# Another way of turning a 128-row tile upside down, and a later place for the transform that reads it

## The chip, the cores and the metric

The kernel runs on one core of one Trainium2 chip. The metric is device time in microseconds (us) of one launch, from the first to the last instruction of the program and a little around it. The engines are PE (matrix multiplications, with PEld for its weight loads), DVE, ACT and POOL (elementwise work) and SP, which here only issues DMA transfers. Each engine works through its own list of instructions in order; semaphores make it wait for others.

## The reference, cut to what matters

Three stages follow each other on a batch of 2 sequences of 768 tokens with 512 features. The first is a linear attention with decay (blocks of 64 tokens). The second is this, and the change lies in it:

```
X = np.fft.fft(x, axis=1)            # over the 768 tokens
X = np.fft.fft(X, axis=2)            # over the 512 features
mixed = np.real(X)
u = x + mixed
un = (u - mean(u)) / sqrt(var(u) + 1e-06)
x = u + np.maximum(un @ w_ch1, 0.0) @ w_ch2      # 512 -> 2048 -> 512
```

The third is a second MLP of the same size with its own normalisation. All inputs and outputs are float32; the kernel carries most products as pairs of float16 (a high part and the rest).

## The kernel before, in words

The tokens of a sequence are cut into six tiles of 128. `U[b][j]`, j from 0 to 5, holds the attention's output of sequence b; tiles 3 to 5 hold the mirrored half of the tokens. The real part of a two-dimensional Fourier transform is symmetric, so the kernel adds and subtracts mirrored tokens and mirrored features first ("fold") and multiplies by smaller cosine and sine tables. For sequence 1 it folds once more over the tokens: tile 0 of the folded rows is added to and subtracted from tile 2 with its rows in reverse order. This reversed copy is the tile `turned` (z in the code): row 0 of z is zero, and row p is row 128 - p of the folded tile 2. [...] `fold_mid` (L585) folds tile 1, `fold_both` (L588 to L595) folds tile 0, copies half a row into it (L590), and makes `radd` and `rsub` (L593); each is split into a float16 pair `fadd`, `fsub` by ACT (L563) and POOL (L564).

`dft1_two` (L609 to L636) multiplies these pairs by the token tables, in five groups g of output columns (L622, L627, L630), and ACT and DVE copy the sums out as `cst` (L635, L636). `dft2_q` (L672) and `dft2_x` (L656, L658) transform over the features into `ps_pq`, three tiles j, and `add_cos` (L691) adds the result to U. Then come the statistics (L777 to L796), the normalised rows `un` and their pair `uns` (L797 to L806), and a DMA transpose into `unT` (L808), from which the MLP's first product of block 2 reads.

This work runs beside the MLP of the blocks that are ready. The MLP is cut into units n of one block and one sixteenth of the 2048 features: `mlp_up` (L843) makes `ps_h`, ACT and DVE turn it into the pair h (L857, L858), and `mlp_down`, three units later, multiplies h by the second weights into `ps_y` (L1003). A table `bg` says which background task is emitted in which unit: `put(n, task)` rounds n down. A task emitted there is a piece of program; a scheduler then sets the order on PE, DVE, ACT and POOL by its own estimate of times, and instructions may end up somewhat before or after their unit. DMA issues that wait for nothing on an engine can stand much earlier. SP issues all transfers of this part in one list, and waits in it for the data of each.

The lines that set the places are these (L1455 to L1464):

```
n = t + DC + DFO                 # 22
put(n - 2, fold_turn)
put(n, fold_mid)
put(n, fold_both)
n += DD                          # 22.5
for i, g in enumerate((2, 3, 4, 0, 1)):
    put(n + i * D1S, lambda g=g: dft1_two(g, bk1))     # D1S = 0.5
n += 4 * D1S + 1
```

`w1_sums` (L876 to L888) prepares sums of the first weights on DVE, ACT and POOL and has no part in the transform; its instructions `wr`, `ws` and `sw` stand between the others.

Of the kernel before, what the change touches and what calls it, by code (L numbers as in the profile page):

```python
# [11 lines left out]
F32 = mybir.dt.float32  # L12
# [7 lines left out]
P = 128  # L20
B, H, S, D = 2, 8, 768, 64
DM, DF = 512, 2048
# [29 lines left out]
EARLY0, GATEN, B1, SPC, DS, DC, DFO, DD, D1S, D2S, AO, YA, NR, NE, LN1, L1, L2, F01, F02, TL, R1, R2, SE, PR1, LAG, UB, FB, NW, MQ, SPL = 11, 8, 6, 2.0, 2.0, 5, 1.0, 0.5, 0.5, 1.0, "aba", "aa", 2, 0, 3, 2.5, 2.5, 16, 4, 3, 1.5, 2, "dddd_dppp", 0, 3, 3, 13, 11, 1, 3  # L52
# [22 lines left out]
def split16(a):  # L75
    hi = a.astype(np.float16)
    lo = (a - hi.astype(np.float64)).astype(np.float16)
    return hi, lo


def shape_tables():
    t = np.arange(TB)
    s = np.arange(NS)
    ang = 2.0 * np.pi * ((t[:, None] * s[None, :]) % S) / S
    cs = np.cos(ang) * TS
    sn = np.sin(ang) * TS
    d = np.arange(P)
    dd = np.arange(ND)
    cd = np.cos(2.0 * np.pi * ((d[:, None] * dd[None, :]) % DM) / DM) * TS
    dse, dso = d[:, None] * dd[None, 2:-1:2], (d[:, None] + 1) * dd[None, 1::2]  # L90
    sd = np.sin(2.0 * np.pi * (np.concatenate([dso, dse], 1) % DM) / DM) * TS
    sd[P - 1, :P] *= 0.5

    def lay(a, n):
        parts = [x.reshape(n, P, -1).transpose(1, 0, 2) for x in split16(a)]
        return np.ascontiguousarray(np.stack(parts, 1))

    def full(a, n):
        return np.ascontiguousarray(a.astype(np.float32).reshape(n, P, -1).transpose(1, 0, 2))

    even, odd = np.arange(0, DM, 2), np.arange(1, DM, 2)
    wide = np.stack([np.cos(2.0 * np.pi * (d[:, None] * even % DM) / DM), np.cos(2.0 * np.pi * (d[:, None] * odd % DM) / DM),
                     -np.sin(2.0 * np.pi * (d[:, None] * even % DM) / DM), -np.sin(2.0 * np.pi * ((d[:, None] + 1) * odd % DM) / DM)], 1) * TS
    wide[0, 2] = np.where(even % 4, -0.5, 0.5) * TS
    wide[P - 1, 3] *= 0.5
    so = np.concatenate([np.arange(0, NT, 2), np.arange(1, NT, 2)])
    tc = np.cos(2.0 * np.pi * (t[:2 * P, None] * so % S) / S) * TS
    ss = so[so < TB]
    ts = np.sin(2.0 * np.pi * (t[:2 * P, None] * ss % S) / S) * TS
    ts[0] = np.sin(2.0 * np.pi * (2 * P * ss % S) / S) * TS  # L110
    r3 = np.round(2.0 * np.cos(2.0 * np.pi * (2 * P * so % S) / S)) / 2
    cr4 = np.stack([np.where(so % 2, -2.0, 0.0)] * 2 + [r3] * 2) * TS

    def two(a, n):
        return np.ascontiguousarray(np.stack([x.reshape(2, P, n).transpose(1, 0, 2) for x in split16(a)], 1))

    n = np.arange(P)
    expo = np.zeros((P, H + 8 + P), np.float32)
    expo[:, :H] = n[:, None]
    expo[:, H:H + 4] = P  # L120
    for i, m in enumerate((n < D, n >= D, n > 0, n == 0)):
        expo[:, H + 4 + i] = m
    expo[:, H + 8:] = np.eye(P)
    return {
        "cs2": two(tc, NT),
        "sn2": two(ts, TB),
        "cr4": cr4.astype(np.float16),
        "cs": lay(cs, 3),
        "sn": lay(sn[:, :TB], 3),
        "cd": lay(np.concatenate([cd[:, ::2], cd[:, 1::2]], 1), 1)[:, :, 0],  # L130
        "sd": lay(sd, 1)[:, :, 0],
        "cr": ((np.where(s % 2, -1.0, 1.0) - 1.0) * TS).astype(np.float16)[None],
        "dr": np.tile(np.where(dd[::2] % 4, -0.5, 0.5) * TS, (2, 1)).astype(np.float16),
        "cs32": full(cs, 3),
        "sn32": full(sn[:, :TB], 3),
        "wide": wide.astype(np.float32),
        "expo": expo,
    }
# [3 lines left out]
def tile_retention_fourier_mlp(ctx: ExitStack, tc: tile.TileContext, a: dict, out: bass.AP):  # L142
    nc = tc.nc
    pe, act, dve, pool, sp = nc.tensor, nc.scalar, nc.vector, nc.gpsimd, nc.sync
# [12 lines left out]
    dram = ctx.enter_context(tc.tile_pool(name="dram", bufs=1, space=DRAM))  # L157
# [5 lines left out]
    def bank(which, name):  # L163
        return banks[which].tile([P, 512], F32, tag=which, name=name)

    def f32t(name, spare=None):
        if spare is not None:
            return wpool.tile([P, 512], F32, tag=f"w2_{spare}", name=name)
        return fp.tile([P, 512], F32, tag="f", name=name)
# [386 lines left out]
    def fold_two(m):  # L556
        run(fold_half(1, m, 1, pool))
        run(fold_half(1, m, 0))
        return folds[1, m][2]
# [9 lines left out]
    def fold_turn():  # L569
        f = fold_two(2)  # L570
        t = f32t("r256").bitcast(F16)[0:1].rearrange("p (two n) -> p two n", two=2)[:, :, :ND]
        act.copy(t[:, 0], f[0:1, :ND])
        pool.tensor_tensor(t[:, 1], f[0:1, :ND], t[:, 0], op=ALU.subtract)
        sp.dma_start(rows4[1][2:4], t)
        z = turned["f"] = f32t("turned")
        pool.memset(z[0:1], 0.0)
        d, e = (dram.tile([P, DM], F32, name=f"turned_{x}") for x in "de")
        sp.dma_start(d, f)
        x_, y_ = d[:], e[:]
        halves_of = [[DM // 2, 2], [DM, P - 1], [1, DM // 2]]  # L580
        sp.dma_start(bass.AP(y_.tensor, y_.offset + DM, halves_of),
                     bass.AP(x_.tensor, x_.offset + (P - 1) * DM, [[DM // 2, 2], [-DM, P - 1], [1, DM // 2]]))
        sp.dma_start(z[1:P], e[1:P])

    def fold_mid():  # L585
        fhl[1, 1] = pair_of_rows(fold_two(1), "fm1")
# [25 lines left out]
    def dft1_two(g, bk):  # L612
        c0, w, tn, _ = GRP[g]
        cos = tn == "cs"
        n = NT // 2 if cos else HB
        t = tab[tn + "2"]
        ps = bank(bk["d"], f"ps_d1_{g}")
        todo = [(1, slice(0, 2 * n), 1), ("add" if cos else "sub", slice(0, n), 0), ("sub" if cos else "add", slice(n, 2 * n), 0)]
        if w > 1:
            for nm, o, m in todo:  # L620
                for i, (x, y) in enumerate(PASS):
                    pe.matmul(ps[:w, o], fhl[1, nm][:, x, c0:c0 + w], t[:, y, m, o], start=nm == 1 and i == 0,  # L622
                              stop=not cos and nm == "add" and i == 2, skip_group_check=True)
        else:
            for y in range(2):
                for nm, o, m in todo:
                    pe.matmul(ps[:2 - y, o], fhl[1, nm][:, :2 - y, c0], t[:, y, m, o], start=nm == 1 and y == 0, stop=False,  # L627
                              skip_group_check=True)
        if cos:
            pe.matmul(ps[:w, :2 * n], rows4[1][:, c0:c0 + w], tab["cr4"], start=False, stop=True, skip_group_check=True)  # L630
        w = max(w, 2)
        t = cst[1, g] = csp.tile([P, 2, NT], F16, tag=f"cs{g}", name=f"cst1_{g}")
        hi, lo = (t[:w, x, :2 * n].rearrange("p (i e) -> p e i", e=2) for x in range(2))
        z = ps[:w, :2 * n].rearrange("p (e i) -> p e i", e=2)
        act.activation(hi, z, AF.Copy, scale=CS)  # L635
        dve.scalar_tensor_tensor(lo, z, CS, hi, op0=ALU.mult, op1=ALU.subtract)  # L636
# [682 lines left out]
    bk1 = {"a": "at", "s": "at", "i": "at", "o": "at", "st": "at", "d": "at", "l": "at", "p": "at"}  # L1319
# [110 lines left out]
    def put(n, task):  # L1430
        bg.setdefault(max(int(n), 0), []).append((n, len(bg), task))
# [21 lines left out]
    for c in range(NCH):  # L1453
# [3 lines left out]
        put(t + DC, lambda c=c: (attn_i(1, c, bk1), attn_c(1, c, bk1)))  # L1457
    n = t + DC + DFO
    put(n - 2, fold_turn)
    put(n, fold_mid)  # L1460
    put(n, fold_both)
    n += DD
    for i, g in enumerate((2, 3, 4, 0, 1)):
        put(n + i * D1S, lambda g=g: dft1_two(g, bk1))  # L1464
    n += 4 * D1S + 1
    for j in range(3):
        put(n + j * D2S, lambda j=j: (run(dft2_q(1, j, bk1)), run(sub_sin(1, j)), dft2_x(1, j), ln_a(0, 2, j)))
# [99 lines left out]
```

## Time and profile before

| | us |
|---|---|
| median of 3 runs (589.07 to 590.15) | 589.98 |
| the profiled execution's own time | 588.64 |
| its span, first to last instruction | 586.9 |
| PE busy in it | 561.4 |

The trace is of one execution, and its times count from the start of its span. A line of the timeline is: start, time taken, engine, line of the program, operation, output from input, and in brackets how long the engine sat idle before and what ended that. A line of the chain of waits is: start, time, and what the program's end hung on in that time.

### The profile page before, as it was taken

What the parts mean: (1) busy time and instruction counts of PE and PEld (TensorE: products, weight loads), DVE (VectorE), ACT (ScalarE), POOL (GpSimd) and SP (SyncE); (2) the same over time, 40 slices, a digit from 0 to 9 for tenths busy, and PEclk for the clock granted to TensorE, in tenths of its full rate; (3) what the DMA queues carried; (4) which work ended last, traced back from release to release, by engine and by line L of the source; (5) the groups of instructions that cost most, each with busy time, mean ns of one, the idle gap of its engine ahead of it and who ended that gap; (6) DMA issues with size and microseconds to landing.
All of it is one profiled execution on the core that took longest, in us unless ns stands there. A gap on an engine that the chain in (4) does not pass through costs nothing.

```text
span 586.9 us, 12192 instructions
## 1 busy us (share of the span) xinstructions
PE 561.4 (96%) x4700; PEld 384.5 (66%) x4700; DVE 403.9 (69%) x917; ACT 302.7 (52%) x621; POOL 335.5 (57%) x355
## 2 busy tenths in 40 slices
PE   7979999999995999989999899999999999999997
PEld 4746555566552554666677677776777778878885
DVE  6897896787864447888687866557656665756544
ACT  4867888733232232645688788954243454322320
POOL 7826599976442353655367678764096676223511
PEclk9999999999997999999999999999999999999999
DMA  8997089950010010244265443510120125002101
GB/s 282 407 412 278 23 274 252 330 182 3 1 43 12 1 36 20 58 111 152 73 166 181 144 162 115 167 27 1 55 55 1 18 88 59 1 1 75 37 1 55
DMA packets 47417, 63.92 MB, mean 109 GB/s; under 512 B 26236, under 2 KB 29183, under 8 KB 47358
## 3 DMA queue, kind: packets, MB, share of 16 engines
q1 hardware_dynamic: 46542, 62.92, 34.6%
q8 instruction: 37, 0.61, 0.4%
q10 hardware_dynamic: 816, 0.21, 0.2%
q14 instruction: 22, 0.18, 0.1%
HBM read 52.63 MB, written 6.81 MB: 101 GB/s over the span
## 4 chain that ended last, share of the span: by engine, by line
PE 62%; DVE 13%; ACT 8%; POOL 6%; DMA 6%; issue 5%; SPq 0%; DVEq 0%; POOLq 0%; ACTq 0%
PE ps_y L1003 25%; PE ps L952 21%; PE ps_h L843 5%; DVE wr L876 2%; DMA turned<-turned_e 2%; PE ps_y L1050 2%; POOL m L393 1%; DMA turned_e<-turned_d 1%; PE ps_a L1050 1%; PE ps_b L1050 1%; POOL w L343 1%; PE ps_s L381 1%; ACT top L324 1%; ACT w L341 1%; DMA ws<-in_w 1%
## 5 line engine op out<-in xcount | busy, mean ns | idle before, releaser
L1003 PE MATMUL ps_y<-w,h 128*128 128x512 f16 (+1 forms) x1026 | 249.4, 378 | 2.7 <-DVE h L989 1.6
L1003 PEld LDWEIGHTS <-h 128*128 128x128 f16 x1032 | 98.0, 98 | 89.5 <-ACT h L988 2.7
L952 PEld LDWEIGHTS <-sw 128*128 128x128 f16 x1104 | 94.6, 98 | 21.7 <-issue 3.3
L952 PE MATMUL ps<-th,sw 128*128 128x192 f16 x756 | 86.0, 246 | 2.1 <-DVE s L969 1.2
L343 POOL TENSOR_TENSOR w<-wf,w 128x512 f16<-128x512 f32 x58 | 66.9, 1160 | 32.3 <-ACT w L341 32.2
L952 PEld LDWEIGHTS <-w 128*128 128x128 f16 x828 | 70.9, 98 | 11.0 <-issue 0.8
L843 PE MATMUL ps_h<-unT,w 128*128 128x384 f16 x396 | 72.8, 328 | 1.8 <-DVE h L858 1.7
L952 PE MATMUL ps<-unT,w 128*128 128x192 f16 x552 | 61.6, 246 | 0.0
L843 PEld LDWEIGHTS <-w 128*128 128x128 f16 x396 | 38.0, 98 | 30.7 <-issue 3.2
L888 POOL TENSOR_TENSOR sw<-ws,sw 128x512 f16<-128x512 f32 x32 | 36.9, 1167 | 18.4 <-ACT sw L887 18.3
L341 ACT CAST w<-wf 128x512 f16<-128x512 f32 x58 | 35.1, 611 | 10.1 <-DVE wf L328 7.2
L1238 ACT ACTIVATE h<-ps 128x384 f16<-128x384 f32 x44 | 21.7, 496 | 34.6 <-DVE ps L1245 30.0
L917 POOL TENSOR_TENSOR th<-ts,th 128x384 f16<-128x384 f32 x22 | 20.2, 936 | 27.1 <-ACT th L916 27.1
L318 DVE SCALAR_TENSOR_TENSOR wf<-ws,ps_w 128x512 int32<-128x512 int32 x34 | 23.2, 684 | 17.1 <-ACT ps_w L316 6.7
L393 POOL TENSOR_TENSOR m<-m,m 128x512 f16<-128x512 f32 x24 | 31.6, 1332 | 5.6 <-ACT m L391 3.6
L785 POOL TENSOR_TENSOR rs<-rs,neghalf 128x1 f32<-128x1 f32 x24 | 13.5, 567 | 34.8 <-DVE rs L783 34.8
L1267 POOL TENSOR_TENSOR hh<-s,hh 128x256 f16<-128x256 f32 x22 | 14.4, 677 | 32.9 <-ACT hh L1266 30.9
L806 POOL TENSOR_TENSOR uns<-un,uns 128x512 f16<-128x512 f32 x21 | 25.4, 1207 | 13.5 <-ACT uns L805 13.5
L988 ACT ACTIVATE h<-ps 128x384 f16<-128x384 f32 x48 | 22.4, 487 | 20.5 <-DVE ps L982 18.6
L989 DVE SCALAR_TENSOR_TENSOR h<-ps,h 128x384 f16<-128x384 f32 x48 | 25.4, 553 | 10.6 <-ACT h L988 10.0
L857 ACT ACTIVATE h<-ps_h 128x384 f16<-128x384 f32 x36 | 17.1, 482 | 25.7 <-PE ps_h L843 25.7
L952 PE MATMUL ps<-unT,sw 128*128 128x192 f16 x276 | 30.3, 246 | 0.0
(248 smaller groups left out, 1031.5 us busy)
## 6 DMA issues: line engine op xcount, KB each, us to landing
ws<-in_w SPq DMA_DIRECT2D x25, 511.8 KB, 6.3
ws<-in_w2b SPq DMA_DIRECT2D x16, 511.8 KB, 4.3
ws<-in_w1b SPq DMA_DIRECT2D x16, 511.8 KB, 3.9
kt<-in_kt SPq DMA_DIRECT2D x12, 256.0 KB, 3.6
qt<-in_qt SPq DMA_DIRECT2D x12, 256.0 KB, 4.9
v<-in_v SPq DMA_DIRECT2D x12, 256.0 KB
k<-in_k SPq DMA_DIRECT2D x12, 256.0 KB, 5.0
pre<-in_w SPq DMA_DIRECT2D x4, 511.8 KB, 6.9
```

Of the source, the lines that this page charges most:

```text
L318: dve.scalar_tensor_tensor(ti, raw[:, :, 0], 13, part.bitcast(I32), op0=ALU.logical_shift_right, op1=ALU.bitwise_or)
L341: act.copy(hi, t)
L343: gate["lo"] = pool.tensor_tensor(lo, t, hi, op=ALU.subtract)
L393: pool.tensor_tensor(t[:, 1], m32, t[:, 0], op=ALU.subtract)
L806: pool.tensor_tensor(s_[:, 1], un, s_[:, 0], op=ALU.subtract)
L843: pe.matmul(ps, w[:, i, k, fo:fo + P], x[:, j, k, :], start=n == 0, stop=n == 11)
L888: pool.tensor_tensor(lo, z, hi, op=ALU.subtract)
L952: pe.matmul(ps, lhs, rhs, start=start and n == 0, stop=n == 5, skip_group_check=True)
L988: gate["relu"] = act.activation(hi, z, AF.Relu)
L989: dve.scalar_tensor_tensor(lo, z, 0.0, hi, op0=ALU.max, op1=ALU.subtract)
L1003: pe.matmul(ps, h[:, x, j * P:(j + 1) * P], w[:, y, c], start=f == first and n == 0, stop=f == NF - 1 and n == 2, skip_group_check=True)
L1050: pe.matmul(ps[:, c], lhs[:, x], rhs[:, y], start=start == 1 and n == 0 and p == 0, stop=n == 2, skip_group_check=True)
```

## The change: whole rows, eight strips, a later place

The turn keeps its three transfers, with other shapes. `turned_d` gets 129 rows: the 128 of f and behind them a row of zeros, which a transfer of its own brings from a new input `none` (2 KB). The reversing copy starts at that last row and moves 128 rows instead of 127, in eight column strips of 64 numbers (256 bytes) instead of two of 256 numbers (1 KB). The load of z then moves 128 rows instead of 127, and the clearing of z's row 0 on POOL is gone. In the table of tasks the five groups of `dft1_two` go from 22.5, 23, 23.5, 24, 24.5 to 23.5, 23.75, 24, 24.25, 24.5: rounded down, groups 2 and 4 move by one unit each (22 to 23, 23 to 24) and the others stay.

```diff
@@ shape_tables
         "sn2": two(ts, TB),
+        "none": np.zeros((1, DM), np.float32),
@@ fold_turn
         z = turned["f"] = f32t("turned")
-        pool.memset(z[0:1], 0.0)
-        d, e = (dram.tile([P, DM], F32, name=f"turned_{x}") for x in "de")
-        sp.dma_start(d, f)
-        x_, y_ = d[:], e[:]
-        halves_of = [[DM // 2, 2], [DM, P - 1], [1, DM // 2]]
-        sp.dma_start(bass.AP(y_.tensor, y_.offset + DM, halves_of),
-                     bass.AP(x_.tensor, x_.offset + (P - 1) * DM, [[DM // 2, 2], [-DM, P - 1], [1, DM // 2]]))
-        sp.dma_start(z[1:P], e[1:P])
+        d, e = dram.tile([P + 1, DM], F32, name="turned_d"), dram.tile([P, DM], F32, name="turned_e")
+        sp.dma_start(d[P:], a["none"])
+        sp.dma_start(d[:P], f)
+        x_, y_, w = d[:], e[:], DM // 8
+        sp.dma_start(bass.AP(y_.tensor, y_.offset, [[w, 8], [DM, P], [1, w]]),
+                     bass.AP(x_.tensor, x_.offset + P * DM, [[w, 8], [-DM, P], [1, w]]))
+        sp.dma_start(z, e)
@@ the table of tasks
-        put(n + i * D1S, lambda g=g: dft1_two(g, bk1))
+        put(n + 1 + i * D1S / 2, lambda g=g: dft1_two(g, bk1))
```

The scheduler answers to both edits, so the order of the instructions changes from the folds of sequence 1 until some units later; before that PE, DVE, ACT and POOL have the same order. On SP the new transfer of the zero row stands far ahead, behind the load of the table `cr4` and ahead of five weight loads. Line numbers between L127 and L577 are higher by one in the changed kernel.

The first place is PE's list where the transform first reads `fsub`, which is made of `radd`'s partner `rsub`. Before, products for an earlier unit's `ps_y` stand ahead of it:

```order
L1003 MATMUL ps_y_1_2_2372<-w_0_6_1269,h_1_3_2526 128x512
L1003 LDWEIGHTS h_1_3_2526
L1003 MATMUL ps_y_1_2_2372<-w_0_6_1269,h_1_3_2526 128x512
L622 LDWEIGHTS fsub_2562
L622 MATMUL ps_d_2_2565<-sn_1_1922,fsub_2562 128x192
```

Now twelve products of the next unit's `ps_h` and three of the next `ps_y` stand between these and `fsub`:

```order
L843 MATMUL ps_h_1_10_2755<-unT_1_1188,w_0_2_1154 128x384
L843 LDWEIGHTS w_0_2_1154
L843 MATMUL ps_h_1_10_2755<-unT_1_1188,w_0_2_1154 128x384
L1003 LDWEIGHTS h_1_3_2526
L1003 MATMUL ps_y_1_0_2370<-w_0_7_1328,h_1_3_2526 128x512
L1003 LDWEIGHTS h_1_3_2526
L1003 MATMUL ps_y_1_0_2370<-w_0_7_1328,h_1_3_2526 128x512
L1003 LDWEIGHTS h_1_3_2526
L1003 MATMUL ps_y_1_0_2370<-w_0_7_1328,h_1_3_2526 128x512
L622 LDWEIGHTS fsub_2562
L622 MATMUL ps_d_2_2589<-sn_1_1922,fsub_2562 128x192
```

So PE meets `fsub` later in its list, by 12 products of 384 columns and 3 or 4 of 512.

The second place is DVE's list in front of `radd`: e, o and f are the steps of fold 0, h is the pair of a unit of the MLP (here those of `ps_h_1_7` and `ps_h_1_8`). Before:

```order
L858 SCALAR_TENSOR_TENSOR h_1_3_2526<-ps_h_1_7_2587,h_1_3_2526 128x384
L537 TENSOR_TENSOR e_0_2543<-e_0_2543 128x255
L540 TENSOR_TENSOR f_0_2545<-e_0_2543 128x128
L541 TENSOR_TENSOR f_0_2545<-e_0_2543 128x129
L535 TENSOR_TENSOR o_0_2544<-u_120 128x512
L537 TENSOR_TENSOR o_0_2544<-o_0_2544 128x255
L543 TENSOR_TENSOR f_0_2545<-o_0_2544 128x127
L544 TENSOR_TENSOR f_0_2545<-o_0_2544 128x128
L858 SCALAR_TENSOR_TENSOR h_1_4_2648<-ps_h_1_8_2635,h_1_4_2648 128x384
L593 TENSOR_TENSOR radd_2555<-f_0_2545,turned 128x512
```

Now:

```order
L538 TENSOR_TENSOR e_0_2543<-e_0_2543 128x255
L858 SCALAR_TENSOR_TENSOR h_1_4_2637<-ps_h_1_8_2624,h_1_4_2637 128x384
L541 TENSOR_TENSOR f_0_2545<-e_0_2543 128x128
L542 TENSOR_TENSOR f_0_2545<-e_0_2543 128x129
L536 TENSOR_TENSOR o_0_2544<-u_120 128x512
L538 TENSOR_TENSOR o_0_2544<-o_0_2544 128x255
L544 TENSOR_TENSOR f_0_2545<-o_0_2544 128x127
L545 TENSOR_TENSOR f_0_2545<-o_0_2544 128x128
L593 TENSOR_TENSOR radd_2555<-f_0_2545,turned 128x512
```

The h of `ps_h_1_8` has moved from behind fold 0 into it, so six of the fold's steps now wait behind that h.

The third place is PE's list at the last piece of the feature transform, `ps_pq_2`, from which the last third of block 2's rows is made. Before, its last product is followed by three products for `ps_h_1_15` and then 36 for `ps_y`, up to the first product of block 2:

```order
L656 MATMUL ps_pq_2_2865<-cdsd,cst_1_2676 128x128
L843 LDWEIGHTS w_0_3_1379
L843 MATMUL ps_h_1_15_2991<-unT_1_1188,w_0_3_1379 128x384
L843 LDWEIGHTS w_0_3_1379
L843 MATMUL ps_h_1_15_2991<-unT_1_1188,w_0_3_1379 128x384
```

Now it is followed by 32 for `ps_y` alone:

```order
L656 MATMUL ps_pq_2_2865<-cdsd,cst_1_2676 128x128
L1003 LDWEIGHTS h_1_6_2915
L1003 MATMUL ps_y_1_1_2371<-w_0_12_1682,h_1_6_2915 128x512
L1003 LDWEIGHTS h_1_6_2915
L1003 MATMUL ps_y_1_1_2371<-w_0_12_1682,h_1_6_2915 128x512
```

Seven products (three of 384 and four of 512 columns) have moved from behind it to in front of it.

## Rows read from the trace of the kernel before

**Rows 1.** The page, part 1: busy time, share of span and count of each engine.
```profile
PE 561.4 (96%) x4700; PEld 384.5 (66%) x4700; DVE 403.9 (69%) x917; ACT 302.7 (52%) x621; POOL 335.5 (57%) x355
```

**Rows 2.** Windows of 10 us: length, busy time and count by engine, PE's clock, DMA share, GB/s.
```profile
180.00:190.00 10.00, 4.61 (x22) 2.56 (x22) 6.28 (x9) 2.92 (x6) 3.65 (x3) 0.66 0.02 7
```

**Rows 3.** Waits of the whole span: who for whom, us in total, times, longest.
```profile
DVE radd L593 <- DMA turned<-turned_e: 9.4, 1, 9.4
```

**Rows 4.** Timeline, 155 to 215 us, all engines, columns as told above.
```profile
155.62 0.52 POOL L576 MEMSET turned<- 1x512 f32 x1
...
157.58 0.67 POOL L573 TENSOR_TENSOR r<-f,r 1x257 f16<-1x257 f32 x1 [1.45 <-ACT r L572]
157.86 1.54 DVE L876 TENSOR_TENSOR wr<-w 128x512 f32<-128x512 f16 x2
...
160.53 0.28 DVE L544 TENSOR_TENSOR f<-o 128x128 f32<-128x128 f32 x1
...
171.33 0.29 DVE L540 TENSOR_TENSOR f<-e 128x128 f32<-128x128 f32 x1
...
171.93 0.49 ACT L857 ACTIVATE h<-ps_h 128x384 f16<-128x384 f32 x1 [1.76 <-PE ps_h L843]
...
173.44 0.40 ACT L590 COPY f<-f 1x255 f32<-1x255 f32 x1 [1.02 <-DVE f L544]
...
176.80 1.55 PEld L1003 LDWEIGHTS <-h 128*128 128x128 f16 x8
...
185.31 0.82 PE L622 MATMUL ps_d<-sn,fsub 128*128 128x192 f16 x4 [6.45 <-ACT fsub L563]
...
186.21 0.08 PEld L627 LDWEIGHTS <-fadd 128*2 128x2 f16 x1 [0.46 <-POOL fadd L564]
```

**Rows 5.** Chain of waits, 150 to 240 us: start, time, what.
```profile
160.83 1.98 DMA turned_d<-f
...
162.83 7.99 DMA turned_e<-turned_d
...
170.84 12.32 DMA turned<-turned_e
...
187.07 1.28 PE ps_h L843 x4
...
193.73 0.65 PE ps_h L843 x4
...
217.52 0.49 PE ps_h L843 x3
218.00 7.77 PE ps_y L1003 x36
```

**Rows 6.** Windows of 1 us, columns as in rows 2.
```profile
167.00:168.00 1.00, 1.00 (x8) 0.59 (x6) 1.00 (x3) 0.00 (x0) 0.00 (x0) 1.00 0.14 49
...
174.00:175.00 1.00, 1.00 (x6) 0.39 (x5) 0.00 (x0) 0.00 (x0) 0.00 (x0) 1.00 0.07 27
...
183.00:184.00 1.00, 0.00 (x0) 0.00 (x0) 0.75 (x2) 0.03 (x1) 0.00 (x0) 0.50 0.00 0
...
188.00:189.00 1.00, 1.00 (x8) 0.81 (x6) 0.96 (x3) 0.30 (x1) 0.00 (x0) 0.50 0.00 0
189.00:190.00 1.00, 1.00 (x8) 0.50 (x6) 0.59 (x2) 1.00 (x3) 0.60 (x1) 0.76 0.00 0
```

**Rows 7.** DMA issues by line: tensors, queue, count, KB each, median us to landing.
```profile
w<-wd SPq DMA_DIRECT2D x6, 256.0 KB, 3.9
```

**Rows 8.** Window of 40 to 50 us, columns as in rows 2.
```profile
40.00:50.00 10.00, 9.77 (x41) 4.79 (x40) 8.13 (x20) 6.71 (x15) 5.11 (x5) 1.00 1.00 364
```

**Rows 9.** Timeline, DVE, 215 to 231 us.
```profile
220.14 0.54 DVE L858 SCALAR_TENSOR_TENSOR h<-ps_h,h 128x384 f16<-128x384 f32 x1
```

**Rows 10.** Timeline, weight loads, 224 to 231 us.
```profile
225.69 3.69 PEld L843 LDWEIGHTS <-w 128*128 128x128 f16 x24 [0.41 <-DMA unT<-uns]
```

**Rows 11.** Timeline, PE, 240 to 270 us.
```profile
251.11 0.39 PE L1003 MATMUL ps_y<-w,h 128*128 128x512 f16 x1 [1.58 <-DVE h L989]
```

## Prediction

> **What bounds the kernel now.** I read the page first. PE is busy for 96% of the span, and no other engine is over 69% [rows 1], so what counts is where PE is idle or slow, and in the windows one stretch stands out: from 180 to 190 us PE is busy 4.61 us of 10 and its granted clock is 0.66 [rows 2]. The list of waits names the cause: DVE waits 9.4 us, once, for the load of `turned` [rows 3]. The timeline shows what that costs PE: its last products start at 176.80, and at 185.31 it has been idle 6.45 us for `fsub`; one instruction later its weight load waits 0.46 us more for POOL's `fadd` [rows 4]. The chain of waits shows the three transfers of the turn one behind the other: 1.98 us for the store, 7.99 for the reversing copy, 12.32 for the load, 22.3 in all from 160.83 to 183.16 [rows 5]. All three move about 256 KB, so the shape makes the difference. The 1 us windows say how: during the reversing copy the DMA engines are busy 0.14 of 16, that is 2.2 engines, at 49 GB/s; during the load 0.07, that is 1.1 engines, at 27 GB/s [rows 6]. A copy whose outer count is 2 ran on about two engines, a load of 127 rows on about one.
>
> **The transfers now.** The store of 128 rows took 1.98 us and stays. DVE's list brings it forward: `wr`, `wr` (1.54 us) and two `ws` stood ahead of f's last step, which began at 160.53 [rows 4], and now stand behind it. That is some 2 us, so f is done at about 158.7 and the store lands at 160.9. The load of 128 rows has the shape of the store, mirrored: not under its 1.98 us [rows 5], not over the 3.9 us that another 256 KB load from DRAM takes as a median [rows 7]. I take 2.5, nearer to the store, as the queue is as empty here.
>
> The reversing copy has no row of its own. Before, at 49 GB/s two engines moved 48 pieces of 1 KB per us, some 45 ns for a piece on one engine; of the 7.99 us about 5.7 were pieces (127 for each of two engines) and 2.3 start and landing. Now there are 8 x 128 pieces of a quarter of that size. On eight engines, 128 pieces each cost between a quarter of 45 ns (1.4 us) and the full 45 ns (5.8 us): 3.7 to 8.1 us with the 2.3. I take 6, and z lands at 160.9 + 6 + 2.5 = 169.4, with 166.6 and 172.9 as the ends.
>
> The windows show two and one engine but never eight, so the step from eight strips to eight engines is not in the trace. The Trainium skill ("DMA: Bandwidth & Descriptors", section "Why a DMA increments its semaphore by 16 and not by 1") has a rule: a transfer issued from SP runs on the largest number of engines, 16 at most, that divides the outer counts of both sides. It gives 2 and 1 for the two shapes before, as the windows show, and 8 and 16 for those of now; by it the sum is the one worked out here. If the strips ran on two engines as before, the copy would take between 512 x 11 ns + 2.3 = 8.1 us and 512 x 45 ns + 2.3 = 25.3 us; the upper end is a rival below.
>
> **What is late next.** `radd` needs z, but also fold 0 with its half row from ACT. Before, ACT's copy of that half row began at 173.44 [rows 4], 9.4 us before z came, so the turn was the only late one. Now fold 0 waits inside itself for the h of `ps_h_1_8`, whose ACT half begins at 171.93 and takes 0.49 [rows 4]: with DVE's half (0.54 by the same instruction at [rows 9]) the fold's last six steps start at about 172.95 instead of 171.33, and the half row ends at 173.84 + 1.6 = 175.45. So `radd` starts at about 175.5, and z has been there for 2.6 to 9 us. PE reached `fsub` at 178.85 (185.31 less 6.45) [rows 4]. Its list now has 12 products of 0.1625 us (0.65 for four) and four of 0.216 (7.77 for 36) [rows 5] more ahead of it: 178.85 + 1.95 + 0.86 = 181.7. Before, 2.15 us passed from z's landing to the first product with `fsub`; ACT now puts an h between the two casts, 0.5 us, so `fsub` is there at 178.2, and `fadd`'s rest, 3.0 us behind z before, at 178.5. PE waits for neither; 3 us are to spare.
>
> **The sum.** The stall goes: 6.45 us. The wait for `fadd` goes: 0.46 us. And the clock: PE's granted clock was 1.00 until the stall, 0.50 (1.2 of 2.4 GHz) at 183 to 189 us and 0.76 in the next [rows 6]; four `ps_h` took 1.28 us there, 0.65 us six us later [rows 5]. PE was busy 4.61 us in this [rows 2], 3.61 at half rate and 1.00 at 0.76: at the full clock 1.81 + 0.24 = 2.05 us less, 1.6 if the smallest products don't shrink. I take 2.0. Together 8.9 us.
>
> Against it stands the third place in the order. Block 2's first product follows its transposed rows without slack: its weight load already waited 0.41 us for them [rows 10]. The products of `ps_pq_2`, where these rows begin, are now followed by 32 products instead of 39, so PE arrives 3 x 0.1625 + 4 x 0.216 = 1.35 us sooner. On DVE an h of 0.54 us, begun at 220.14 [rows 9] between the statistics of these rows, now stands ahead of them, which gives back 0.45. PE should wait 0.9 us there. DVE does not wait for it: it works on the drains and statistics of other blocks, and a while later PE waits 1.58 us for DVE [rows 11], a wait that shrinks by what DVE gains. So the loss is between 0 and 1.35; I take 0.5.
>
> At nothing: the clearing on POOL (0.52 us), behind which POOL sat idle 1.45 us [rows 4]. The zero row's transfer is issued at some 43 us, when the DMA engines are busy 1.00 [rows 8] and the queue is not what the loads wait for; if SP's list were the bound there, its slot of about 0.4 us would be lost. The transform's groups have the same products as before.
>
> The gain is 8.9 - 0.5 = 8.4 us: 588.64 would become 580.2. The median shown is 1.34 us above the profiled execution's own time, so the forecast is 589.98 - 8.4 = 581.6 us.
>
> **The rivals.**
> First, more is given back. For it: from 225 us on the scheduler's new order touches all engines until some 260 us, with no slack at block 2's start [rows 10] and DVE late soon after [rows 11]. Against it: DVE meets `radd` 3 us earlier in PE's list than before, so it has no new backlog. Price: the whole 1.35 at block 2, and the 1.58 again: 589.98 - 8.9 + 1.35 + 1.58 = 584.0.
>
> Second, the late DVE of rows 11 recovers wholly, since it is not stopped by the turn: no loss at block 2 and up to 1.58 more: 579.5.
>
> Third, the change doesn't do what it says: the turn stays as late as it was, because pieces of 256 bytes cost as much as pieces of 1 KB and the strips fall on two or three engines. With 20 us for three transfers instead of 22.3 the stall shrinks by what PE has more to do and no more; 588 to 591.
>
> Fourth, slower: the strips run on two engines at 45 ns a piece, 25.3 us. z lands at 160.9 + 25.3 + 2.5 = 188.7 and `fsub` is there at 191.3; PE has waited since 181.7, 9.6 us instead of 6.9, again with the slow clock after it, and the 0.5 at block 2 is lost as well: 589.98 + 2.7 + 0.5 = 593.2. It decides from a copy of some 14 us: then z lands at 177.4, behind fold 0 by more than the time to spare for `fsub`'s rest.
>
> **How the numbers follow.** Forecast 0.66, its own range 580.3 to 583.0 (no loss to 1.35 at block 2, 1.6 for the clock). First rival 0.17, second 0.08, third 0.04, fourth 0.05. A difference of 0.2%, 1.2 us, is about what a measurement of this kernel can tell from none. Faster: forecast, first and second, 0.91. Same: 0.04. Slower: 0.05. The range from 579.2 to 585.6 takes the second rival and most of the first, and leaves out the last two.
>
> **What would show it.** In the profile after, the chain has no DMA of the turn; the load of z takes 2 to 4 us and the copy 4 to 8, at a DMA share near 0.5 while it runs. `radd` waits for ACT's half row (L590), not for a transfer. PE is never idle for more than 0.5 us between 170 and 200 us and its clock stays 1.00. PE or its weight load waits about 1 us for `unT` at block 2's first product. The forecast is wrong if a 1 us window shows the copy at 0.14 again, or if the stall is gone and the time has fallen by less than 5 us.

## The result and the profile after

The changed kernel took 579.75 us (median of 4 runs, 578.53 to 581.00) beside 589.86 us for the kernel before on the same chip: ratio 0.9831, 95% interval 0.9805 to 0.9857. That is 10.1 us faster; the forecast was 581.6 with a range of 579.2 to 585.6.

The profiled execution took 580.48 us, its span is 578.7 (before: 588.64 and 586.9). The page's first part shows PE at the same work in a shorter span [rows 1]:

```profile
PE 561.9 (97%) x4700; PEld 385.5 (67%) x4700; DVE 402.3 (70%) x917; ACT 301.7 (52%) x621; POOL 335.8 (58%) x354
```

The windows (length, busy time and count by engine, PE's clock, DMA share, GB/s) answer to [rows 2, 6]:

```profile
100.00:110.00 10.00, 8.26 (x44) 4.27 (x44) 6.50 (x10) 6.48 (x13) 8.53 (x8) 0.83 1.11 356
...
165.00:166.00 1.00, 1.00 (x8) 0.58 (x6) 0.00 (x0) 0.11 (x1) 0.00 (x0) 1.00 0.63 144
...
180.00:190.00 10.00, 10.00 (x62) 5.51 (x61) 7.07 (x12) 4.25 (x9) 5.32 (x4) 1.00 0.00 0
```

The stretch from 180 to 190 us, 4.61 us busy at 0.66 before, is now full at 1.00. The reversing copy runs at a DMA share of 0.63 where it had 0.14. The first row is a disturbance of this one execution: the clock is at 0.83 near 105 us, where PE waits a little in every execution (1.00 in the kernel before's). The same products start at 154.96 us before and at 156.70 here, so by then all is 1.74 us later, and the times below contain that. It is no cost of the change: e4 below has the same order and the same zero row, and stands 0.2 us ahead of the kernel before there.

The timeline at the turn answers to [rows 4, 5]. SPq is the issue of a transfer: the store of the folded tile f to DRAM as `turned_d`, the copy with rows reversed to `turned_e`, and the load into z.

```profile
160.80 0.34 SPq L579 DMA_DIRECT2D turned_d<-f  x1
162.79 0.72 SPq L581 DMA_DIRECT2D turned_e<-turned_d  x1
166.76 0.33 SPq L583 DMA_DIRECT2D turned<-turned_e  x1
...
169.57 1.36 DVE L538 TENSOR_TENSOR e<-e 128x255 f32<-128x255 f32 x1 [2.27 <-POOL e L536]
...
178.64 0.69 DVE L593 TENSOR_TENSOR radd<-f,turned 128x512 f32<-128x512 f32 x1 [0.47 <-ACT f L590]
...
180.27 0.61 ACT L564 CAST fsub<-rsub 128x512 f16<-128x512 f32 x1
...
183.25 0.49 PE L622 MATMUL ps_d<-sn,fsub 128*128 128x192 f16 x4
```

The store takes 1.99 us from issue to the next issue, the copy 3.97 instead of 7.99, the load 2.6 from issue to landing instead of 12.3, so z is there at 169.4. `radd` waits for ACT's half row and not for a transfer, and PE reads `fsub` without a wait, 2.4 us after its cast. The chain of waits has no transfer of the turn any more.

The timeline of PE from 214 to 262 us has two waits, and answers to [rows 10, 11]:

```profile
219.76 4.06 PE L843 MATMUL ps_h<-unT,w 128*128 128x384 f16 x24 [0.88 <-DMA unT<-uns]
256.22 0.66 PE L952 MATMUL ps<-th,sw 128*128 128x192 f16 x6 [0.66 <-DVE s L969]
```

Block 2 starts 0.88 us late. The wait of 1.58 us for DVE's h [rows 11] is gone, and so is one that the kernel before had ahead of it:

```profile
245.95 0.66 PE L952 MATMUL ps<-th,w 128*128 128x192 f16 x6 [0.45 <-DVE t L976]
```

### The profile page after: what moved, and what is told of

The parts are those of the page before. It is cut to its first block, busy times and chain, and to the rows that moved or that the text cites. A ratio compares the mean times of both kernels' runs of the same rounds, so it can differ in the third digit from the quotient of the medians.

```text
span 578.7 us, 12188 instructions
## 1 busy us (share of the span) xinstructions
PE 561.9 (97%) x4700; PEld 385.5 (67%) x4700; DVE 402.3 (70%) x917; ACT 301.7 (52%) x621; POOL 335.8 (58%) x354
## 4 chain that ended last, share of the span: by engine, by line
PE 43%; DVE 4%; POOL 3%; issue 3%; ACT 3%; POOLq 0%; ACTq 0%
PE ps L952 20%; PE ps_y L1003 18%; PE ps_y L1050 2%; PE ps_a L1050 1%; PE ps_b L1050 1%; POOL w L344 1%; DVE tr L899 1%; DVE wf L319 1%; ACT h L988 0%; ACT half L316 0%; DVE ts L920 0%; POOL sw L888 0%; ACT wf L341 0%; ACT ps_w L317 0%; ACT th L916 0%
## 5 line engine op out<-in xcount | busy, mean ns | idle before, releaser
L785 POOL TENSOR_TENSOR rs<-rs,neghalf 128x1 f32<-128x1 f32 x24 | 13.7, 577 | 31.5 <-DVE rs L783 31.5
L797 ACT ACTIVATE un<-u,rs 128x512 f32<-128x512 f32 x24 | 19.5, 813 | 21.0 <-DVE rs L796 17.8
```

## The experiments

All kernels were timed beside the kernel before on their own chip: e1 to e4 on one, e5 to e8 on a second, e9 and e10 on a third. So ratios are compared across the three groups, and medians within one. Two traces with the same order can also be compared product by product on PE, which is finer than either. The open question after the result was which of the edits pays: the transfers, the order of the instructions, or the place in the table of tasks. Two facts of the order helped to separate them. With the new line in the table alone the order stays that of before, and with the old line and the new turn it is that of the changed kernel, instruction for instruction on all five engines. What turns the order over is the clearing of z's row 0 on POOL: with it the old order comes (e1, e9, e10), without it a new one, in two versions: the changed kernel, e4 and e5 have the first, e2 and e6 the second.

### e1: new turn, old order

```diff
+        pool.memset(z[0:1], 0.0)
         sp.dma_start(z, e)
```

> The changed kernel with the clearing of z's row 0 on POOL put back (the load then writes that row again). With it PE, DVE, ACT and POOL have the order of the kernel before throughout; the transfers are the changed kernel's. Theory (the gain is z's earlier arrival): f's store leaves at 160.8 us, z lands at 169.4, radd starts when ACT's half row is there, about 174.5, fsub is ready by about 177 and PE, which reaches it at 178.85, doesn't wait. Median 589.9 - 8.9 = 581.0, and about 579 if DVE's late waits near 251 us go as well, because they were the stall's backlog. Rival (the new order of the instructions is the gain, by putting 2.8 us of other products ahead of fsub): most of the stall stays away only with that order, so at least 585.

Measured: 581.28 us, ratio 0.9875 (0.9862 to 0.9889). From its timeline:

```profile
174.12 0.69 DVE L594 TENSOR_TENSOR radd<-f,turned 128x512 f32<-128x512 f32 x1
...
178.93 0.49 PE L623 MATMUL ps_d<-sn,fsub 128*128 128x192 f16 x4
```

Neither waits. The stall is gone without the new order, so the rival falls. Its late waits of PE:

```profile
218.06 4.06 PE L844 MATMUL ps_h<-unT,w 128*128 128x384 f16 x24 [0.68 <-DMA unT<-uns]
...
238.31 0.66 PE L953 MATMUL ps<-th,w 128*128 128x192 f16 x6 [0.45 <-DVE t L977]
...
243.63 0.39 PE L1004 MATMUL ps_y<-w,h 128*128 128x512 f16 x1 [1.75 <-DVE h L990]
```

The waits for DVE are still there, as long as before (0.45 and 1.58 us) or a little longer, although DVE was never stopped by the turn. So they are no backlog of the stall: they belong to the old order. DVE's timeline in front of that h shows why:

```profile
240.91 2.14 DVE L877 TENSOR_TENSOR wr<-w 128x512 f32<-128x512 f16 x2 [1.05 <-DMA unT<-uns]
...
243.04 1.01 DVE L990 SCALAR_TENSOR_TENSOR h<-ps,h 128x384 f16<-128x384 f32 x2
```

and the same place in the changed kernel:

```profile
241.03 1.29 DVE L876 TENSOR_TENSOR wr<-w 128x512 f32<-128x512 f16 x2
...
242.31 1.00 DVE L989 SCALAR_TENSOR_TENSOR h<-ps,h 128x384 f16<-128x384 f32 x2
```

In the old order `wr` waits 1.05 us for a transposing transfer that reads `uns` (both tiles come from one pool of buffers) and stands ahead of the h that PE wants; in the new order it doesn't wait. That the waits belong to the order is shown by the runs. That the buffer is the cause is only read from these rows and the code: no kernel with buffers of its own for `wr` was run.

### e2: old turn, new order

```diff
-        pool.memset(z[0:1], 0.0)
         d, e = (dram.tile([P, DM], F32, name=f"turned_{x}") for x in "de")
...
         sp.dma_start(z[1:P], e[1:P])
+        sp.dma_start(z[0:1], a["none"])
```

> The kernel before, with z's row 0 loaded from the zero row in place of POOL's clearing: the turn is still the old one (two strips, 127 rows, 22.3 us), the place of the groups is the old one, but the order of the instructions is nearly the changed kernel's. Theory (z's arrival against the time at which PE reaches fsub): f is done some 1.8 us sooner, z lands at about 181.4, fsub is ready at 183.5, PE is there at 181.5 and waits 2 us, with a short slow clock behind it: 582 to 583.5. Rival (the order is the whole gain): 579.8. Rival (the transfers are the whole gain, the order none): 589.9.

Measured: 585.72 us, ratio 0.9956 (0.9942 to 0.9969): none of the three numbers. From the timeline:

```profile
181.56 0.69 DVE L594 TENSOR_TENSOR radd<-f,turned 128x512 f32<-128x512 f32 x1 [6.37 <-DMA turned<-turned_e]
...
183.60 0.50 PE L623 MATMUL ps_d<-sn,fsub 128*128 128x192 f16 x4 [2.65 <-ACT fsub L564]
...
184.52 0.25 PE L628 MATMUL ps_d<-cs,fadd 128*2 128x193 f16 x1 [0.41 <-POOL fadd L565]
...
186.08 0.34 PE L623 MATMUL ps_d<-sn,fsub 128*128 128x192 f16 x1 [0.82 <-POOL fsub L565]
```

z and `fsub` came within 0.2 us of the expected times, but PE was there 0.5 us sooner, and POOL's rests were late too: 3.88 us idle, not 2. The windows show the rest of it:

```profile
185.00:186.00 1.00, 0.26 (x2) 0.00 (x0) 1.00 (x3) 0.00 (x0) 1.00 (x1) 0.55 0.00 0
186.00:187.00 1.00, 0.92 (x6) 0.88 (x7) 0.98 (x3) 0.00 (x0) 0.03 (x1) 0.50 0.00 0
187.00:188.00 1.00, 1.00 (x7) 0.46 (x6) 0.43 (x1) 0.99 (x2) 0.29 (x1) 0.50 0.00 0
...
191.00:192.00 1.00, 1.00 (x4) 0.34 (x3) 0.00 (x0) 0.00 (x0) 0.00 (x0) 0.53 0.00 0
```

Four rows are like 187 to 188, at 1.2 of 2.4 GHz. Busy time by what the clock lacks: 0.26 x 0.45 + 0.92 x 0.5 + 4 x 0.5 + 0.47 = 3.05 us. A stall of 3.88 us cost more clock than the 6.9 us of before, because there the slow stretch began while PE still waited [rows 6], and here it fell on full work. The sum can be checked against e6 below, which has the same order and no stall. On PE the two traces stand together at 161.2 us; behind the slow stretch, where `ps_h` begins at 192.06 here and at 185.02 there, e2 is 7.0 us behind, and 3.88 + 3.05 is 6.9. The rest of the difference of their spans (584.6 and 576.8) is block 2's first product, for which PE waits 1.35 us here and 0.67 in e6:

```profile
225.62 4.06 PE L844 MATMUL ps_h<-unT,w 128*128 128x384 f16 x24 [1.35 <-DMA unT<-uns]
```

The new order is worth 3.1 us with the slow turn (588.86 - 585.72) and 2.7 with the quick one (e1 against e4, 581.28 - 578.61). Of these 2.7 the late waits of PE explain 2.0 (0.68 + 0.45 + 1.75 in e1, 0.85 in e4); 0.4 us more lies ahead of the turn in the two traces.

### e3: the later place alone

```diff
-        put(n + i * D1S, lambda g=g: dft1_two(g, bk1))
+        put(n + 1 + i * D1S / 2, lambda g=g: dft1_two(g, bk1))
```

> The kernel before with the changed kernel's line in the table of tasks alone (groups at n + 1 + i / 4). The scheduler's order on PE, DVE, ACT, POOL and SP comes out as that of the kernel before. Theory: no change, 589.9 within 0.2%. Rival (the later place takes part in the gain): 585 to 588.

Measured: 589.11 us, ratio 1.0009 (0.9997 to 1.0020). No change, and PE's stall at `fsub` is there:

```profile
185.34 0.82 PE L622 MATMUL ps_d<-sn,fsub 128*128 128x192 f16 x4 [6.62 <-ACT fsub L563]
```

The place alone gives nothing.

### e4: a load of 127 rows in the changed kernel

```diff
-        sp.dma_start(z, e)
+        sp.dma_start(z[1:P], e[1:P])
+        sp.dma_start(z[0:1], e[0:1])
```

> The changed kernel with its load of z cut into rows 1 to 127 and row 0: same order on PE, DVE, ACT and POOL, same store and copy, but the load of 127 rows, 12.3 us in the kernel before. Theory: z lands at about 177.3 (179.1 where the early clock dip of the profiled run shifts all by 1.7), radd starts 0.5 us later than in the changed kernel, fsub is there about 2 us before PE: 579.8, no change. Rival (every us of the turn counts, 22.3 - 8.6 = 13.7 us saved for 10): 9.7 us more in the load give back some 5 to 7 us, 585 to 587.

Measured: 578.61 us, ratio 0.9832 (0.9819 to 0.9846), the same as the whole change. From the timeline:

```profile
177.59 0.69 DVE L594 TENSOR_TENSOR radd<-f,turned 128x512 f32<-128x512 f32 x1 [1.35 <-DMA turned<-turned_e]
...
181.32 0.49 PE L623 MATMUL ps_d<-sn,fsub 128*128 128x192 f16 x4
```

DVE waits 1.35 us for the transfer again, and PE for nothing. Ten of the 13.7 us by which the turn got shorter are worth nothing in the new order.

### e5: new turn, old place

This is e3's line undone in the changed kernel, the two lines above with - and + exchanged.

> The changed kernel with the old line in the table of tasks: the turn's part alone. The order on PE, DVE, ACT, POOL and SP comes out as that of the changed kernel. Theory (the place does nothing, the turn's edits make both the transfers and the order): ratio 0.983, as the whole change. Rival (the place is needed with the new turn): above 0.986. Its spread is of interest too: runs with a granted clock of 1.000 near 578.5, runs at 0.994 to 0.997 up to 2 us above them, by the dip near 105 us.

Measured: 579.16 us, ratio 0.9848 (0.9832 to 0.9863). Its interval overlaps that of the whole change, and by the times alone e5 leaves room for a few tenths of a per cent. The traces settle it: with the same order on PE, e5's products stand 1.41 us ahead of the changed kernel's at 162 us and 1.43 at the end (the dip near 105 us is missing here). From the turn on the two run alike, so the place does nothing. Of the spread nothing is learned: its slowest run, 579.54 us, has a granted clock of 0.999.

### e6: two strips

```diff
-        x_, y_, w = d[:], e[:], DM // 8
+        x_, y_, w = d[:], e[:], DM // 2
```

and 2 for 8 in the two patterns.

> The changed kernel with two strips of 1 KB pieces in the reversing copy, whole rows everywhere: the copy should take 8 us as in the kernel before, the load 2.6. Its order has the clearing gone too and equals that of the run with the old turn and new order. Theory: z lands 4 us later than in the changed kernel, near 171.5 us, and radd still waits for ACT's half row, not for z: no loss, ratio 0.983, so the eight strips are not needed. Rival (the strips are the gain): at least half of the 4 us shows, ratio 0.987 or more.

Measured: 578.15 us, ratio 0.9831 (0.9816 to 0.9847). From the timeline:

```profile
161.15 0.64 SPq L581 DMA_DIRECT2D turned_e<-turned_d  x1
169.41 0.33 SPq L583 DMA_DIRECT2D turned<-turned_e  x1
...
175.65 0.69 DVE L593 TENSOR_TENSOR radd<-f,turned 128x512 f32<-128x512 f32 x1 [0.47 <-ACT f L590]
```

The copy takes 8.26 us and `radd` still waits for ACT. The eight strips aren't needed here. The order differs a little from the changed kernel's, so this run alone changes two things; e10 shows the same with the old order.

### e7: the feature transform half a step apart

```diff
-        put(n + j * D2S, lambda j=j: (run(dft2_q(1, j, bk1)), ...
+        put(n + j * D2S / 2, lambda j=j: (run(dft2_q(1, j, bk1)), ...
-        put(n + 1 + j * D2S, lambda j=j: (ln_n(0, 2, j), ...
+        put(n + 1 + j * D2S / 2, lambda j=j: (ln_n(0, 2, j), ...
```

> The changed kernel with the three tiles of the feature transform and their statistics half a unit apart in the table of tasks in place of one, so that the products of ps_pq_2 and its successors come earlier among the other products (six products for ps_h and one for ps_y move behind). Theory: PE's wait of 0.88 us for unT at block 2's first product shrinks or goes, and the rest stays: ratio 0.9815 to 0.983. Rival (the scheduler's order of the late stretch shifts again and DVE's late waits of the order before come back): 0.985 or more.

Measured: 578.59 us, ratio 0.9838 (0.9823 to 0.9854). PE's wait for `unT` is 0.88 us to the digit. The edit didn't do what it was for: in its trace, too, 32 products for `ps_y` stand between the last product of `ps_pq_2` and block 2's first, as in the changed kernel, and only earlier pieces of the feature transform have moved. So the run doesn't test whether these products make the wait. What would remove it stays open.

### e8: the shapes by themselves

```diff
+    sp.dma_start(dst(1, 128, 2), src(0, 128, 2))     # strips of a reversed copy: rows, count
+    sp.dma_start(dst(1, 127, 2), src(0, 127, 2))
+    sp.dma_start(dst(1, 127, 8), src(0, 127, 8))
...
+    sp.dma_start(pt, pd[5])
+    sp.dma_start(pt[0:127], pd[5][0:127])
...
```

> The changed kernel with a chain of transfers behind its last output, each waiting for the one before: from a store of 128 rows, reversing copies between DRAM tensors (2 strips x 128 rows, 2 x 127, 8 x 127, then 4, 8, 16 and 32 strips x 128), then loads into one tile of 128, 127, 126, 124, 122, 120 and 112 rows of 2 KB. Its end is later by all of these. Theory (the number of engines is the largest up to 16 that divides the outer counts, pieces of 1 KB cost 45 ns on an engine): copies of 2 strips 8 us, 4 strips 5, 8 strips 4, 16 and 32 strips 3 to 4, and 127 rows like 128 where strips stand outside; loads: 128 and 112 rows 2 to 2.6 us, 127 rows 12.3, 126 rows (14 engines) under 3, 124 (4) 4.5, 122 (2) 7, 120 (15) under 3. Rival (127 rows are slow because their count is odd or their last piece is uneven): 126, 124 and 122 rows all under 3. Rival (smaller pieces cost as much as large ones): from 8 strips on the copy gets slower again, 16 strips 6 us, 32 strips 9 us.

From SP's timeline, where each issue waits for the transfer before it: L1555 is 2 strips of 128 rows, L1556 2 of 127, L1557 8 of 127, L1558 to L1561 are 4, 8, 16 and 32 strips of 128, L1562 to L1568 the loads of 128, 127, 126, 124, 122, 120 and 112 rows.

```profile
...
596.88 0.58 SPq L1558 DMA_DIRECT2D p<-p  x1
602.45 0.62 SPq L1559 DMA_DIRECT2D p<-p  x1
606.54 0.58 SPq L1560 DMA_DIRECT2D p<-p  x1
610.12 0.55 SPq L1561 DMA_DIRECT2D p<-p  x1
615.18 0.32 SPq L1562 DMA_DIRECT2D pt<-p  x1
617.89 0.26 SPq L1563 DMA_DIRECT2D pt<-p  x1
630.48 0.32 SPq L1564 DMA_DIRECT2D pt<-p  x1
633.09 0.24 SPq L1565 DMA_DIRECT2D pt<-p  x1
637.88 0.23 SPq L1566 DMA_DIRECT2D pt<-p  x1
645.13 0.32 SPq L1567 DMA_DIRECT2D pt<-p  x1
647.87 0.31 SPq L1568 DMA_DIRECT2D pt<-p  x1
```

Windows of 1 us in the loads of 127, 124 and 122 rows, in this order (columns as in [rows 2]):

```profile
622.00:623.00 1.00, 0.00 (x0) 0.00 (x0) 0.00 (x0) 0.00 (x0) 0.00 (x0) 0.50 0.06 25
...
635.00:636.00 1.00, 0.00 (x0) 0.00 (x0) 0.00 (x0) 0.00 (x0) 0.00 (x0) 0.50 0.24 76
...
641.00:642.00 1.00, 0.00 (x0) 0.00 (x0) 0.00 (x0) 0.00 (x0) 0.00 (x0) 0.50 0.12 47
```

| 256 KB or a little less | us, issue to next issue |
|---|---|
| copy, 2 strips x 128 rows; x 127 | 8.14; 8.21 |
| copy, 4 strips | 5.57 |
| copy, 8 strips x 128; x 127 | 4.09; 4.09 |
| copy, 16 strips; 32 strips | 3.58; 5.06 |
| load, 128 rows; 127; 126 | 2.71; 12.59; 2.61 |
| load, 124 rows; 122; 120 | 4.79; 7.25; 2.74 |

127 rows are slow, and 126 are as quick as 128. In between the times fall as the largest divisor up to 16 says (1 for 127, 2 for 122, 4 for 124, 14 to 16 for the rest), and the DMA share while they run is 0.06, 0.12 and 0.24, that is 1, 2 and 4 of 16 engines: the first rival falls. The Trainium skill ("DMA: Bandwidth & Descriptors", section "Why a DMA increments its semaphore by 16 and not by 1") has this rule of divisors, and these loads agree with it row by row. The second rival falls up to 16 strips; with 32 strips (64-byte pieces) the copy does get slower again, 5.06 instead of the expected 3 to 4 us. The run's 653.02 us hold this chain and say nothing else.

### e9: the eight-strip copy alone, old order

The clearing on POOL is back, and `sp.dma_start(z[1:P], e[1:P])` loads z as before.

> The kernel before's order on PE, DVE, ACT and POOL (row 0 cleared on POOL), with the new store and the eight-strip copy, but the old load of 127 rows: of the 13.7 us that the turn is shorter by, the copy's 4.1 alone. z lands at 167.2 + 12.6 = 179.8 us, so PE, which is at fsub at 178.85, waits 3 us for fsub, then 0.4 for fadd's rest and some 0.5 for fsub's rest: 3.9 us in place of 6.9. Theory (the clock's cost depends on where the slow stretch falls, not on the length of the stall): the clock falls late in these waits, as in the run with the old turn and the new order, so the slow stretch lies on busy time and costs 3 us in place of 2.0, and POOL's wait is new: before minus 0.5 to 2, ratio 0.9965 to 0.999. Rival (the slow clock's cost shrinks with the stall): before minus 3.0 minus 1 to 2, ratio 0.9915 to 0.993.

Measured: 585.73 us, ratio 0.9943 (0.9922 to 0.9963), between the two. From the timeline and the windows:

```profile
179.51 0.69 DVE L594 TENSOR_TENSOR radd<-f,turned 128x512 f32<-128x512 f32 x1 [5.44 <-DMA turned<-turned_e]
...
181.57 0.50 PE L623 MATMUL ps_d<-sn,fsub 128*128 128x192 f16 x4 [2.51 <-ACT fsub L564]
...
182.48 0.33 PE L628 MATMUL ps_d<-cs,fadd 128*2 128x193 f16 x1 [0.40 <-POOL fadd L565]
```

```profile
182.00:183.00 1.00, 0.60 (x3) 0.21 (x3) 0.97 (x1) 0.00 (x0) 1.00 (x2) 0.66 0.00 0
183.00:184.00 1.00, 1.00 (x4) 0.45 (x3) 1.00 (x1) 0.00 (x0) 0.98 (x1) 0.50 0.00 0
...
185.00:186.00 1.00, 1.00 (x8) 0.67 (x7) 0.86 (x2) 1.00 (x2) 0.34 (x1) 0.63 0.00 0
```

PE idles 2.91 us, and the slow stretch is shorter than e2's (the row left out is like 183 to 184): 0.60 x 0.34 + 2 x 0.5 + 0.37 = 1.6 us lost. Product by product the account closes: e9 and e1 have the same order, stand together ahead of the stall (`ps_h` at 175.22 and 175.25 us), and behind it are 4.66 us apart (185.82 and 181.16 for the same product), beside 2.91 + 1.6 = 4.5. But what I expected of the clock was wrong by half, and the rival's rule (less stall, less clock) doesn't carry from e2 either. The eight runs themselves spread from 584.9 us at a mean clock of 0.997 to 588.4 at 0.991; one was traced, so how the others differ isn't shown. What sets the length of the slow stretch stays open.

### e10: the whole-row load alone, old order

The clearing is back, the copy has two strips, all moves have 128 rows.

> The kernel before's order again (row 0 cleared on POOL), two strips as before but whole rows, so the copy keeps its 8.2 us and the load of 128 rows takes 2.7 in place of 12.6. Theory: z lands at 163.05 + 8.2 + 2.65 = 173.9 us, radd waits for ACT's half row until 174.1 anyway, PE never waits for fsub: the whole gain of the run with the old order and the new turn, ratio 0.9875. Rival (every us of the turn counts): two thirds of it, ratio 0.991.

Measured: 580.54 us, ratio 0.9846 (0.9821 to 0.9872). The gain is that of e1: the two have the same order, and e10's products stand 0.54 us ahead of e1's at 161 us already and 0.56 at the end, so what it is better by lies ahead of the turn. From its timeline:

```profile
173.79 0.69 DVE L594 TENSOR_TENSOR radd<-f,turned 128x512 f32<-128x512 f32 x1 [0.22 <-DMA turned<-turned_e]
...
243.05 0.39 PE L1004 MATMUL ps_y<-w,h 128*128 128x512 f16 x1 [1.75 <-DVE h L990]
```

z is late by 0.22 us, and PE doesn't feel it; the old order's late wait for h is there as in e1. A load of whole rows is enough to remove the whole stall.

## Why the prediction was right, and where it wasn't

**What bounds the kernel**: right. With z there in time the stall, the wait for `fadd` and the slow clock are gone in e1, e4 to e7 and e10, and where z is late they come back (e2, e9).

**The transfers**: z lands at 169.4, as forecast, but by luck, through two errors that cancel. The copy took 4.0 us, not 6 (pieces of 256 bytes are nearer to a quarter of the price than I took), the load 2.6 (2.5 forecast). The store left at 160.80, not 158.7; of these 2.1 us 1.74 are the early dip of this execution: in e4, whose order on DVE is the same, it left at 158.88.

**What is late next**: right in kind, `radd` waits for ACT's half row. It starts at 178.64 instead of 175.5, 1.74 of it the dip. Most of the rest I put down to POOL, which the working left out, without a run that tests it: at 169.57 DVE waits 2.27 us for POOL's `e` in fold 1, and fold 0 comes behind that. PE had 2.4 us to spare, 3 forecast.

**The stall and the clock, 6.45 + 0.46 + 2.0**: right, a little too large. From 160 us to block 2's first product the changed kernel is 225.69 - 219.76 + 1.74 = 7.67 us quicker; with the 0.88 that it waits there the stretch saved 8.55, 8.9 forecast. e1 has the order of before and can be laid beside it product by product: it is 0.24 us behind ahead of the stall (161.31 and 161.07 us) and 8.39 ahead after the slow stretch (181.16 and 189.55), 8.63 in all. Less the two waits of 6.91 that leaves 1.7 for the clock, where I took 2.0; the working's lower figure of 1.6 was nearer. That the clock's share is real shows in e2 and e9, where only idle time plus the lost clock gives the measured distance to a run without the stall.

**Block 2, 0.5 lost**: this term was mis-sized, and so was its reason. PE does wait 0.88 us (0.9 forecast), but with the old order it waits 0.64 to 0.68 too as soon as the stall is gone or shorter (e1, e9, e10), so the third place in the order makes about 0.2 of it. Nor does the order alone set this wait: e2 and e6 have the same one and wait 1.35 and 0.67. And not 0.4 but 2.3 us came back later: from block 2's first product to the end the kernel before needs 586.9 - 225.69 = 361.21 us and the changed one 578.7 - 219.76 = 358.94, mainly because the waits of 1.58 and 0.45 us for DVE are gone. So this term is 0.88 - 2.27 = -1.4 instead of +0.5, 1.9 us better; less the 0.35 that stall and clock gave less, these are most of the 1.8 us by which the time lies below the forecast. The second rival named this gain, but for a reason that falls. It held that DVE recovers because the turn no longer stops it; in e1 and e10 the turn doesn't stop it either, and PE still waits 1.75 us for it. The new order removed the wait, and the order came from leaving out the one-row clearing on POOL.

**The numbers of the forecast**: 579.75 lies below the forecast's own range, 580.3 to 583.0. The wider range holds it because it was stretched to 579.2 for the second rival, so that is luck. The terms named for the own range don't give its ends either: 589.98 - 8.9 = 581.1 with nothing lost at block 2, and 589.98 - 8.5 + 1.35 = 582.8. And the third rival's price doesn't follow from its condition: with 20 us for the turn z would land at about 178.9 and `fsub` be there at about 181.5, when PE arrives, so most of the gain would be left. e2 comes nearest to it: the old turn in a new order took 585.7 us, not 588 to 591.

**The place in the table**, told ahead of the prediction as something the scheduler answers to: it has no effect on order or time (e3, e5).

**The fourth rival** (strips on two engines): excluded by the share of 0.63, by the copy's 3.97 us and by e8, where the time falls from 8.14 us for two strips to 5.57 for four and 4.09 for eight.

## What to carry to other kernels

Look at the outer count of a transfer before its bytes: a load of 127 rows took 12.6 us and one of 126 or 128 took 2.7, so choose or pad to a count with a large divisor up to 16. Once a wait has cover, further shortening is worth nothing: of 13.7 us saved on the turn 10 (e4), and in another cut the strips (e6), could be given back free. Before crediting an edit for a gain, split it from the reordering it sets off: here one small clear instruction decided the order of four engines, and that order was worth 2 to 3 us, while the edit that was meant to move things, the later place, did nothing.

## What the hardware showed that I had not expected

A stall of PE doesn't cost the clock in proportion. Idle 6.9 us in two pieces: 1.7 to 2.0 us lost; idle 3.88 us in three pieces: 3.05 us (e2); idle 2.91 us in two: 1.6 us (e9). What these three traces show is that the cost is the work that lies under the slow stretch, and that the stretch need not begin in the first wait: in e2 and e9 the longest single wait was 2.65 and 2.51 us and had ended at 183.60 and 181.57, and the clock fell in the windows from 185 and from 182 us, when PE had worked and waited again.

A copy between DRAM tensors in 16 strips with pieces of 128 bytes was the quickest, 3.58 us for 256 KB; in 32 strips with 64 bytes it took 5.06.
